# Attention and two feed-forward layers on one core: one cleared conversion tile, two score banks, and a new written order

## The chip, the cores and the metric

One core of a Trainium2 chip runs the whole program in one launch. The time is device microseconds from the first to the last instruction of an execution, as the chip reports it; three executions of the kernel before took 922.51, 922.75 and 926.28 us, and their median, 922.75 us, is the time before. The engines are TensorE (PE in the profile, its weight loads PEld), VectorE (DVE), ScalarE (ACT), GpSimd (POOL) and SyncE (SP), which issues the DMA transfers.

## The reference, cut to what matters

Inputs q, k and v are (4, 8, 576, 64) in f32. Attention masks by blocks of 64: a query sees every key of its own block and of the blocks before it. The 2304 rows of 512 that come out go through two feed-forward layers of width 2048.

```python
scores = scale * np.matmul(q, k.transpose(0, 1, 3, 2))
scores = np.where(block_i >= block_j, scores, -1e9)
attn = np.exp(scores - np.max(scores, axis=-1, keepdims=True))
attn = attn / (np.sum(attn, axis=-1, keepdims=True) + 1e-09)
x = np.matmul(attn, v)                       # then (B, S, H*D)
h = x @ w_in;  x = (h * np.tanh(softplus(h))) @ w_out      # layer 1 (Mish)
h = np.maximum(x @ w_in2, 0); out = (h * h) @ w_out2       # layer 2
```

## The kernel before

**Tiles and stages.** The 2304 rows are cut into six chunks of 384 (`CH1`). Chunks 0 and 1 hold the first 192 query positions of the four batches ("lo" attention, `attention_lo`, in f32); chunks 2 to 5 hold the other 384 positions of one batch each ("hi" attention, `attention_hi`, four pairs of heads per chunk, sixteen in all). A pass takes one chunk through one layer (`PASSES`): sixteen slices f of the hidden width, each with a first product (line 1206, into a bank `hp`), an activation, a rounding of the result into two f16 halves (`g_parts`), and a second product (line 1272, into four banks `acc`). Every f16 product is a sum of three matmuls, high by high, low by high and high by low. Pass (0, 0), the first one, runs in f32 instead (lines 1226 and 1241), so that it needs no halves of the weights.

**Weights.** A weight block of 128 x 1024 comes from DRAM 16 bits off its place (line 1053) and is put together in three steps by `decode`: GpSimd clears the target `wf` (line 1058), ScalarE or VectorE converts the upper 16 bits of each number from bf16 to f16 and writes them into the upper halves of the cleared words (lines 1060 and 1061), and VectorE shifts the middle bits by 13 and ORs them in (line 1062, `scalar_tensor_tensor`). There are 16 blocks in each layer. Those of layer 1 stay in tiles of their own (called `first`, `late` and `ws` in the profile), those of layer 2 go through a ring `wf` of three.

**Attention's score banks.** One PSUM tile of two banks (`spare`) holds the hi scores of a pair of heads, one head in each bank (line 833), and, in the last 64 columns of bank 0, small results: scales and norms (`sc`, `qm`, `sx`, `vm`). The lo heads of chunk 1 use the banks in turn (`s1`). For a hi tile VectorE takes the maximum of both heads in one instruction (line 843, `peak`), ScalarE takes the exponential of each head (line 851, `expo`), then P is scaled and rounded to f16 by ScalarE (line 870), VectorE takes the rest of the rounding (line 744), a DMA transposes both halves (line 874), and TensorE multiplies with v (line 931), in bank 0. For a lo head the maxima are lines 972 and 973, the negative scale 974, the exponentials 977, the row scaling 749 or 751, the transposes on TensorE 990 to 993, a copy 720 or 722, and the product with v 1005 and 1006.

**Order.** The program is a list of tasks, and each engine runs its own in a written order. `PLAN` is that list, packed: for every position the task (two bytes, as an offset) and the engine that runs it (one byte). A task with two or three possible engines (`choose`) takes the one that the plan names. The costs in `c_dve`, `c_act` and so on served the search for a plan and do nothing once there is one. Waits between engines are set from what a task reads and writes. SyncE issues the transfers in the plan's order too, so a transfer that waits for its buffer holds those behind it.

Of the kernel before, what the change touches and what calls it, by code (L numbers as in the profile page):

```python
# [59 lines left out]
def seg_len(tiles):  # L60
# [10 lines left out]
       "pn": A + V, "set": A + V, "ptc": A + V, "ph": A + V, "pl": P + V}  # L71
# [23 lines left out]
    "O-K9tG!5Agxm#mhbtj%a+jZ6*MBy==>Dp@v(l@Fbzc=95%~(84*YR1;>MeDz*0SzwyIogd&n&x63y{m%ExHyRe&+XE{P=)=;rb;}_`>R_DIWTaPa}P5pV|!T"
    "u20Zpwq2=-_Mp0Gw=U6lcxVScJYQc~d!484MBo#m`MGV@?K+v6r)#oR(KUL{s%w>&=p){BP!;u7Ro;w8i&J%`PEi|8vR-=I%BvM4Z`mwOWlj~1w-fcX#@TCp"
    "#@gq2;Y7V+BW#R)rE(h03eVUZcB=|&6u%?+JZ;nTx(z0C8WNG0?Q)Gk>Y)AA>T0wO+OyV5AL~sstF7VIOmA2{;=NT*G4dL@{DeKDK<o69J!(TVOb_G1Yw`1N"
    "yMP=UY7dfq9jq^rc+&bHz17ONXY`oeZGF&uJ=c|1%uUl`yNw;rCr`doA8TX3*nQT;YN(UVCjy`7NBahUPt-njw>kEA{XqPBX$Eh)*fn;&-qEqvgX>&tV&xdW"
    "1^;za8?xprS5nLLwJk-<Z_T^Qu)Yad+SIN@_r^BSE+pQKY^WA!tb5-Y*i*VvAKL?(t*3OcjkCAy2|Ym;g&sd&-SJ07eArhf@ca-tQjz#n)Q5QQOlI~`S-pTC"
    "Khzj9t~2vS+gR6v+3%=_dg?_h$om(pmhN>A+s)+qaO;mXrSuTzYJ_gq4DGj5_&#f$bgvC@gKU6R)(|~nZ@D(?`X^#`9n#mk3VPBWu!g!zFS-U=VP(|Q8Z)OZ"  # L100
    "T0F$HnJxo+ZnF*ev=iRFTr;gJ8P$c;c7u9x5>L~`dQ)|fX`x&3#I+i%Zni=_>=yeYS$4ASwkdX&KC`c_E#FggBRN@JpIZwn@9Jn4C$6QP<SroJk9TiaW9zA_"
    "@oiD;YJ!b7U~OrgqoZ`Wovjk&d2vnvej@j-vI6dMJkSb+Y-}G{Rn@mjD(9ZH%gC~eK#!{6S|ioAlfcxqc8*=hsjrBq-T)KoXuWEYGexoVOpxac^6P9nNA=05"
    "3%Fly!$6jEts2>UHt2T{oZDwaj#Uc~!77ZL#A;3*t)v}qd#sclvUcESo|WcX){0qE@TfSR>R|<~h&3bMZ?z1bX%6l^u2C9920y0Pu&zC5yU7M{;`+18RIWdf"
    "y)Tg^Ly61tdK$bK72!%PGOaRqcj^&*Jq3(@p6t1sTzix(ooEk(>|e0zW9p}J_PEB{Kv1VI(*3}pLgd*P*AL`)n#_8N43qBHaI~3bgRtmneQ%HIkbi@_nbuDu"
    "ZJ&Qg53$d8_NE5vIla!)cy{PQPETR|r@-4@>^+7oAFlh|?fSc|@Q-lc6`dFP3E<Z|Amkj*`$?e8mC-8w(D@$SX`?{8ndHq|@X2=`D~QNsPRC%RALN{W=3lkW"
    "`jgt}eQdgi`2%#5TDhU%S0C`9r|u*3o&d3XlKXw_N!_XnWO`#_{JcG)$MN_vWNK-!x+hq9vTjg6B66#H&Ta;q?jVx~Sre=ZXI(|^4gzJ)RTFiEUz+P4aOpM;"
    "09hM=#O*krO<|(CoQuBJ%Ia}KPK1e@AeZB$Gz04|hY7obGfi}<&bNl_KhG}Xlx*XSbO5t{BJ*yr_MGr8WWi<NdVAH<N;04Z*>tw9hEdVP8nA9FID9s`S63Cg"
    "S{K2yGsxlFh*cfcgPR)aHFCWMd~l&12mUrf>X1G|zN9WB7eCVkES^L5ovgE2v4pnTBvs}7O|$z|ll`jW`%5?x@4`f<V)rRl*^bv6c;f&uD@m50t_oI(yg3Wx"
    "D9yWqb_s|*7DTSDqO5QXnQ;)bE<tqvY)6sx#gN=ZwDLf-N0^_rET{8*6*dRY--&MCU!cukp;?~yeAjVuc5=RUlXv@VmoEyJHPd!q3ic_Wtvt`S_CC<_w#(N0"
    "@o4d`wZW&-O>U*_17RC!s<m}**&^SZ{C`kiz)&q+F=A0bvwcC%OIEY|`5<RUcOEFe24))%_Yb9l%ENcdt-cG{zph(?rWbQvXeF3E5)>=W?ls&TYKCjnfZxm9"  # L110
# [24 lines left out]
    "pxO|-IvP!t*osc78_}wzcU>F0sakr{6{8YtsT%ZQHB?&#$euH})`~i*da7&%3<C0J=_tCmlUU#UsoL+&SEMql2_trQ`}`BUk?pZcu<z}zKJ{D=SC88AXxrj9"
    "+bQZ#C$hnB_iwv`cAD0}U}tNP+u-;4U;UY|?NWa%9ncO|UQFFkMulL-(%R|g_&>mGW%ab%;?Lsyq}%9c_{MIKtKru9N8RPr`E9kzpXw^Rer|<d0spV@%lM^A"
    "_b0lm)XpvQf1vv)%l9I81-0L7#v7`k=K3=395>rna5Jc7XZdojgDcMc3?!!eQf``GOAj#9Petw<UleXyPPdVxx2WnCP=_DT=l&Dw6}eA+0e2j4{_eBxV_%tm"
    "Xum%620ztvA24>1%C3o<=nuehV}1PDO=q)<PIE8Z@s{6Bb+=0&+n@b@9S!?!u-E-&jiln(K_|4z3b?hLz~}voej`=z2A$znP{o&^bE`s)T+gjiVS246{0c3y"
    "b$ZM%r5_CYmVy2;YmCOrsm+ga1MEAxpFy1auj$Diu}4Al#(Ef@=w}1qld5hKoIcUb)CAYpK6V%DL-&I|cD;%Gdv3dt+5A?9A2)&KHMPM;yIbu$b+emo20d0c"
    "`x31E(0!*5Tt~RAGd2HwaBvdr@;7&*eWoGo{}sK>$JFfaf_1;Bt+lY%+y`LdKzEl-P)obY-hl-^fP=5Fx2bTO((g?G0WXE${-(=8_xHGt(G4J0eH*LqIZLC|"  # L140
    ")m_BcTv%|ey{tEMzCB@6)dV&^2gdlC>bwT0GW=h-7t|PuGwf8j=SAHIA1%=zVX_yf)$8)M5_mU+r;q5+Ugi4%y~r?iv2%IX*`5N=JK0&_dIv^M=W{>2bvpJ}"
    "hqL-|I){Ksk8*CR*pqYyRjohQ%62@xSRdBz%PD_8{GUB=z5>WNOcTMw+92<7JeB7A1=qfu%{%DTN?UPwqq7QG3C`^xMth-aSDphq$qF&njqaiZIFW%t9;Od!"
    "11}i8i}%;qjqseaj`Toz{(9y7USGsY*&ZtHf}nbF+u@soPt9}<cGu;cH>dY#jxGV**Mhao%Wi=)h9h&xH_$;JSRQND<8D7SdmVoF_)EZm`XJ#>-;fULMzCqC"
# [417 lines left out]
def tile_attention_moe(ctx, tc, qk, qp, va, vd, w1, w2, out):  # L561
# [31 lines left out]
    def fixed(tiles):  # L593
        return sch.ring(len(tiles), lambda i: tiles[i % len(tiles)])
# [184 lines left out]
    def clear():  # L779
# [3 lines left out]
        for z in zeros:  # L783
            for i in R["raw"].insts:
                z.deps.update(i.tasks)
# [810 lines left out]
```

## Time and profile before

| | |
|---|---|
| median of three executions | 922.75 us |
| the profiled execution | 925.42 us, span 923.6 us |
| busy TensorE / VectorE / ScalarE / GpSimd | 895.7 / 575.5 / 575.1 / 63.6 us |
| instructions on them | 5786 / 1432 / 1121 / 86 |
| mean granted TensorE clock | 0.992 of 2.4 GHz |
| DMA | 168.79 MB, 183 GB/s over the span |

A busy microsecond counts an instruction from its start to its end, and that includes time in which it stands on its engine and is held up. Starts are microseconds from the start of the span. In a list of groups the numbers behind the bar are busy us in all, mean ns of one, and the idle time before them with what ended it.

### The profile page before, as it was taken

The page shows a single profiled execution, that of the slowest core. Times are in us where ns is not written, and L with a number is a line of the kernel's source. Part 1 is how long each engine was busy: PE and PEld are TensorE (multiplying, and loading weights), DVE is VectorE, ACT ScalarE, POOL GpSimd, SP SyncE. Part 2 cuts the span into 40 slices and gives each one's busy share as a digit, 9 for nine tenths or more (in the row PEclk, how much of TensorE's full clock was granted, in tenths as well). Part 3 has the DMA queues.
Part 4 walks back from the last instruction along what each step waited for, and adds up shares of the span by engine and source line. Part 5 has one row for each costly group of instructions (what it writes and reads, how often), then busy time and mean ns, then how long its engine had stood idle before and what let it go on. Part 6 is the DMA issues. An engine that isn't in the chain of part 4 may idle for free. (4 is left out here: it accounts for less than half of the span.)

```text
span 923.6 us, 15581 instructions
## 1 busy us (share of the span) xinstructions
PE 895.7 (97%) x5786; PEld 533.2 (58%) x5786; DVE 575.5 (62%) x1432; ACT 575.1 (62%) x1121; POOL 63.6 (7%) x86
## 2 busy tenths in 40 slices
PE   4999999999999999999999999999999999999997
PEld 4666555555555555555566555555666666666664
DVE  6668999999989877586721686976531341331211
ACT  3988899999977655447322786987642333544442
POOL 6000201121211100010000000000000000000000
PEclk8899999999999999999999999999999999999999
DMA  7597556999688899738732388696732222343530
GB/s 272 205 362 288 176 159 156 310 291 290 248 299 198 263 231 234 223 107 199 245 98 83 108 224 211 180 241 160 161 101 70 69 69 69 115 137 137 171 114 35
DMA packets 141772, 168.79 MB, mean 183 GB/s; under 512 B 105856, under 2 KB 110976, under 8 KB 141696
## 3 DMA queue, kind: packets, MB, share of 16 engines
q1 hardware_dynamic: 141696, 167.79, 61.2%
q8 instruction: 45, 0.74, 0.3%
q14 instruction: 31, 0.25, 0.1%
HBM read 125.30 MB, written 17.30 MB: 154 GB/s over the span
## 5 line engine op out<-in xcount | busy, mean ns | idle before, releaser
L744 DVE SCALAR_TENSOR_TENSOR g<-h,cst,g 128x384 f16<-128x384 f32 x176 | 108.7, 619 | 222.4 <-ACT g L1034 218.1
L1212 ACT ACTIVATE h<-hp,cst 128x384 f32<-128x384 f32 x176 | 101.3, 577 | 216.9 <-PE hp L1206 205.7
L1272 PE MATMUL acc<-g,ws 128*128 128x384 f16 x1128 | 228.2, 326 | 0.0
L1272 PE MATMUL acc<-g,raw 128*128 128x384 f16 x984 | 205.2, 326 | 1.6 <-ACT ev L1285 1.6
L1206 PE MATMUL hp<-x,first 128*128 128x384 f16 x768 | 154.8, 326 | 1.0 <-ACT h L1212 0.9
L1272 PEld LDWEIGHTS <-ws 128*128 128x128 f16 x1128 | 108.7, 98 | 72.8 <-issue 2.2
L1272 PEld LDWEIGHTS <-raw 128*128 128x128 f16 x984 | 95.3, 98 | 65.5 <-issue 3.3
L1206 PEld LDWEIGHTS <-first 128*128 128x128 f16 x960 | 92.4, 98 | 63.8 <-issue 3.9
L1206 PE MATMUL hp<-x,raw 128*128 128x384 f16 x552 | 117.9, 326 | 0.0
L1034 ACT ACTIVATE g<-h,cst 128x384 f16<-128x384 f32 x119 | 72.8, 613 | 27.8 <-PE acc L1272 25.6
L1206 PEld LDWEIGHTS <-raw 128*128 128x128 f16 x648 | 61.6, 98 | 40.8 <-issue 1.9
L1206 PE MATMUL hp<-x,ws 128*128 128x384 f16 x408 | 84.7, 326 | 0.4 <-DMA ws<-wspill 0.4
L744 DVE SCALAR_TENSOR_TENSOR pb<-pad,st,pb 128x384 f16<-128x384 f32 (+2 forms) x96 | 71.1, 750 | 13.9 <-ACT pb L870 13.9
L870 ACT ACTIVATE pb<-pad,st 128x384 f16<-128x384 f32 (+2 forms) x96 | 66.4, 713 | 21.3 <-DVE st L863 6.4
L851 ACT ACTIVATE pad<-spare,st,sq 128x448 f32<-128x448 f32 (+1 forms) x96 | 65.1, 680 | 9.8 <-DVE st L846 4.7
L1206 PEld LDWEIGHTS <-ws 128*128 128x128 f16 x504 | 47.8, 98 | 30.8 <-DMA ws<-wspill 0.5
L843 DVE TENSOR_REDUCE st<-spare 128x2 f32<-128x896 f32 (+1 forms) x48 | 47.8, 996 | 10.3 <-PE spare L836 7.6
L1226 PE MATMUL hp<-xs,first 128*128 128x384 f32 x128 | 47.5, 491 | 0.0
L1206 PE MATMUL hp<-late,first 128*128 128x384 f16 x192 | 41.5, 326 | 0.0
L833 PE MATMUL spare<-q 64*128 64x448 f16 (+2 forms) x384 | 38.5, 306 | 1.5 <-ACT pad L851 1.1
L1217 ACT ACTIVATE h<-h 128x384 f32<-128x384 f32 x75 | 38.4, 514 | 0.6
L1241 PE MATMUL acc<-h,late 128*128 128x384 f32 x96 | 36.9, 495 | 0.2 <-ACT h L1231 0.2
(238 smaller groups left out, 1122.9 us busy)
## 6 DMA issues: line engine op xcount, KB each, us to landing
ws<-wspill SPq DMA_DIRECT2D x68, 512.0 KB, 4.6
raw<-wspill SPq DMA_DIRECT2D x68, 512.0 KB, 4.1
raw<-in_w_dram SPq DMA_DIRECT2D x27, 1023.8 KB, 6.5
wspill<-wn SPq DMA_DIRECT2D x24, 512.0 KB, 3.9
qk<-in_qp_dram SPq DMA_DIRECT2D x16, 480.0 KB, 4.6
vs<-in_va_dram SPq DMA_DIRECT2D x16, 320.0 KB, 4.1
pad<-in_w_dram SPq DMA_DIRECT2D x5, 1023.8 KB, 6.8
out_dram<-ev SPq DMA_DIRECT2D x24, 192.0 KB, 2.4
```

The costliest lines, as they stand in the source:

```text
L744: return sch.add("DVE", c_dve(n) + 62 * ap, lambda: nc.vector.scalar_tensor_tensor(dst(), a(), s() if ap else s, c(), op0, op1), r=r, w=w, ...
L833: nc.tensor.matmul(out=pp.t[:, hd, o:o + k1 - k0], lhsT=qh.t[rows, u, a:a + 128], rhs=qh.t[rows, w, nq + k0:nq + k1], start=p == 0, stop=p ...
L843: sch.add("DVE", c_dve(2 * (o1 - o0)), lambda: nc.vector.reduce_max(both(st, j, r0), pp.t[r0:, :, o0:o1], axis=AX.X), w=[(pp, 0), (st, j)])
L851: t = sch.add("ACT", c_act(o1 - o0, True, 3), lambda hd=hd: nc.scalar.activation(pf[hd].t[r0:, k0:k0 + o1 - o0], pp.t[r0:, hd, o0:o1], AF. ...
L870: sch.add("ACT", c_act(n, False, 1), lambda pb=pb, pv=pv, s=s: nc.scalar.activation(pb.t[:, 0:i + 1, 0, :], pv(), AF.Copy, scale=s()), r=[ ...
L1034: "ACT": ("ACT", c_act(n, False, 1), lambda: nc.scalar.activation(dst(0), src(), AF.Copy, scale=s()), False),
L1206: nc.tensor.matmul(out=hp.t[:, 0:n], lhsT=w.t[:, f % 2, a, 128 * k:128 * k + 128], rhs=x.t[:, c, k, 0:n], start=k == 0 and i == 0, stop=k ...
L1212: sch.add("ACT", c_act(n, True, 1), lambda: nc.scalar.activation(h.t[:, 0:n], hp.t[:, 0:n], (AF.Mish, AF.Relu)[l], scale=hs()), r=[(cst, ( ...
L1217: "ACT": ("ACT", c_act(n), lambda: nc.scalar.activation(hv(), hv(), AF.Square), False),
L1226: nc.tensor.matmul(out=hp.t[:, 0:n], lhsT=wf.t[:, 512 * (f % 2) + 128 * k:512 * (f % 2) + 128 * k + 128], rhs=xs.t[:, k, 0:n], start=k == ...
L1241: ts.append(sch.add("PE", c_mm(4 * n), lambda m=m, acc=acc: nc.tensor.matmul(out=acc.t[:, 0:n], lhsT=wf.t[:, 512 * (f % 2) + 128 * m:512 * ...
L1272: nc.tensor.matmul(out=acc.t[:, 0:n], lhsT=wo.t[:, f % 2, a, 128 * m:128 * m + 128], rhs=g.t[:, c, 0:n], start=f == 0 and i == 0, stop=f = ...
```

## The change

Four edits, and a new plan.

```diff
-       "pn": A + V, "set": A + V, "ptc": A + V, "ph": A + V, "pl": P + V}
+       "pn": A + V, "set": A + V, "ptc": A + V, "ph": A, "pl": P + V}
+    top = pad.bitcast(F32)[:, 2048:3072]
+    R["top"] = fixed([top])
...
-    spare = {"ab": psp.tile([128, 2, 512], F32, tag="pab", name="spare")}
-    R["sc"] = fixed([spare["ab"][:, 0, 448 + 4 * i:452 + 4 * i] for i in range(4)])
+    bank = [psp.tile([128, 512], F32, tag=f"bank{i}", name=f"bank{i}") for i in range(2)]
+    R["sc"] = fixed([bank[1][:, 448 + 4 * i:452 + 4 * i] for i in range(4)])
...
+    nc.gpsimd.memset(top, 0.0)
...
-        def peak(st, j, pp, r0, o0, o1):
-            sch.add("DVE", c_dve(2 * (o1 - o0)), lambda: nc.vector.reduce_max(both(st, j, r0), pp.t[r0:, :, o0:o1], axis=AX.X), w=[(pp, 0), (st, j)])
+        def peak(st, j, pp, o0, o1):
+            for hd in range(2):
+                t = sch.add("DVE", c_dve(o1 - o0), lambda hd=hd: nc.vector.reduce_max(st.t[:, 2 * j + hd:2 * j + hd + 1], pp.t[hd][:, o0:o1], axis=AX.X),
+                            w=[(pp, hd), (st, (j, hd))])
...
-                sch.add("ACT", c_act(n, False, 1), lambda pb=pb, pv=pv, s=s: nc.scalar.activation(pb.t[:, 0:i + 1, 0, :], pv(), AF.Copy, scale=s()),
-                        r=[(st, 7), f], w=[(pb, 0)])
+                choose(A + V, {
+                    "ACT": ("ACT", c_act(n, False, 1), lambda pb=pb, pv=pv, s=s: nc.scalar.activation(pb.t[:, 0:i + 1, 0, :], pv(), AF.Copy, scale=s()), False),
+                    "DVE": ("DVE", c_dve(n, True) + 62, lambda pb=pb, pv=pv, s=s: nc.vector.tensor_scalar(pb.t[:, 0:i + 1, 0, :], pv(), s(), None, ALU.mult), True)},
+                    [(st, 7), f], [(pb, 0)])
...
+        top = wf if l else R["top"].new()
+        high = lambda: top.t.bitcast(F16).rearrange("p (c two) -> p c two", two=2)[:, :, 1]
+        if l:
+            sch.add("POOL", 1000.0, lambda: nc.gpsimd.memset(wf.t, 0.0), w=[wf])
...
         sch.add("DVE", c_dve(n), lambda: nc.vector.scalar_tensor_tensor(
-            U(wf.t), mids(), 13, U(wf.t), ALU.logical_shift_right, ALU.bitwise_or), r=[raw], w=[wf], lock=True)
+            U(wf.t), mids(), 13, U(top.t), ALU.logical_shift_right, ALU.bitwise_or), r=[raw, top], w=[wf], lock=True)
```

The layer 1 blocks are converted in one tile `top`, cleared once, and the OR writes the result to its own place; layer 2 keeps its clears. The two score banks are two tiles; maxima and the copy of the tail (line 889) are one instruction per bank; the small results move to bank 1, the product with v stays in bank 0. P's rounding and the scaled copy of the product with v (line 944) may go to either engine.

The plan, unpacked byte by byte, says what it does with the choices. It has 4539 tasks (4491 before): 64 more maxima and tail copies, 16 clears fewer. GpSimd has 48 tasks (80 before), ScalarE 836 (871), VectorE 1541 (1426). Of the 96 roundings of P 24 go to VectorE (7 in chunk 2, 13 in chunk 3, 4 in chunk 4); the copies of line 944 all stay on ScalarE; of the conversions 8 go from ScalarE to VectorE and 2 back; of the row scalings of line 749 17 go to VectorE and 9 back. The changes between the exponential's and Mish's tables on ScalarE are 39 (41 before). Ahead of the first product of pass (0, 0) TensorE has 28 tasks (29 before), ScalarE 47 (57), VectorE 83 (76); GpSimd has seven: three of layer 2's clears and the four small ones of line 962, with the clear of `top` ahead of them (before: nineteen, fifteen of layer 1's clears and the four small ones). The first transposes of TensorE stand behind four score groups (five before).

## Rows read from the trace of the kernel before

**Rows 1.** The page: busy us by engine, and the granted clock in 40 slices.

```profile
PE 895.7 (97%) x5786; PEld 533.2 (58%) x5786; DVE 575.5 (62%) x1432; ACT 575.1 (62%) x1121; POOL 63.6 (7%) x86
...
PEclk8899999999999999999999999999999999999999
```

**Rows 2.** Stages: us, then busy us (count) of PE, PEld, DVE, ACT, POOL, PEclk, DMA share, GB/s.

```profile
11.20:19.30 8.10, 0.00 (x0) 0.00 (x0) 6.21 (x15) 3.81 (x18) 3.80 (x5) 0.75 0.97 375
19.30:29.00 9.70, 9.65 (x40) 8.14 (x41) 3.75 (x19) 7.03 (x30) 0.00 (x0) 0.50 0.35 121
29.00:41.70 12.70, 11.63 (x92) 8.44 (x91) 11.02 (x42) 11.79 (x41) 0.00 (x0) 1.00 0.51 182
41.70:75.00 33.30, 33.04 (x149) 20.55 (x148) 23.82 (x54) 30.01 (x63) 0.00 (x0) 1.00 0.91 338
75.00:225.00 150.00, 147.11 (x867) 84.65 (x866) 143.13 (x343) 140.41 (x236) 23.98 (x30) 1.00 0.80 237
225.00:325.00 100.00, 96.22 (x649) 55.15 (x648) 89.69 (x233) 78.14 (x134) 14.68 (x17) 1.00 0.78 245
325.00:576.00 251.00, 248.31 (x1733) 146.07 (x1730) 157.48 (x408) 133.25 (x272) 5.45 (x7) 1.00 0.66 179
576.00:910.00 334.00, 334.00 (x2182) 198.31 (x2182) 132.42 (x312) 166.04 (x327) 5.03 (x7) 1.00 0.43 125
```

**Rows 3.** Order of time, 6.5 to 15.5 us: start, us, engine, line, what, idle before.

```profile
6.80 8.22 DVE L974 TENSOR_SCALAR st<-st 128x3 f32<-128x3 f32 x1
...
9.58 3.63 POOL L1058 MEMSET first<- 128x1024 f32 x4
...
14.05 0.95 POOL L1058 MEMSET first<- 128x1024 f32 x1
15.12 0.42 ACT L977 ACTIVATE pt<-acc,st 128x192 f32<-128x192 f32 x1 [13.11 <-DVE st L973]
```

**Rows 4.** Order of time on PE alone, 10 to 42 us.

```profile
10.90 0.22 PE L968 MATMUL hp<-never,above 128*128 128x128 bf16 x1
19.35 0.45 PE L990 MATMUL acc<-ident,pt 128*128 128x128 f32 x1 [8.23 <-ACT pt L749]
...
20.23 1.81 PE L967 MATMUL acc<-vs 128*128 128x192 f32 x6
...
30.52 0.98 PE L967 MATMUL spare<-vs 128*128 128x192 f32 x6
...
41.72 1.51 PE L1226 MATMUL hp<-xs,first 128*128 128x384 f32 x4
```

**Rows 5.** Groups of POOL by line and shape: busy us, mean ns, idle before.

```profile
L1058 POOL MEMSET first<- 128x1024 f32 x8 | 7.4, 951 | 0.0
```

**Rows 6.** The same of VectorE.

```profile
L843 DVE TENSOR_REDUCE st<-spare 128x2 f32<-128x896 f32 x32 | 34.7, 1083 | 3.6 <-PE spare L833 1.9 <-PE spare L836 1.2 <-PE spare L807 0.5
...
L1036 DVE TENSOR_SCALAR g<-h,cst 128x384 f16<-128x384 f32 x39 | 16.4, 423 | 14.8 <-PE acc L1272 9.7 <-ACT xs L944 4.0 <-PE spare L1147 0.9
...
L843 DVE TENSOR_REDUCE st<-tl 128x2 f32<-128x256 f32 x16 | 6.6, 410 | 0.0
...
L1061 DVE CAST wf<-raw 128x1024 f16<-128x1024 bf16 x4 | 3.0, 746 | 0.5 <-POOL wf L1058 0.5
```

**Rows 7.** The same of ScalarE.

```profile
L870 ACT ACTIVATE pb<-pad,st 128x512 f16<-128x512 f32 x32 | 22.3, 713 | 5.9 <-DMA late<-pb 2.5 <-ACT pad L851 2.0 <-DMA pt<-pb 0.8
...
L1060 ACT ACTIVATE wf<-raw 128x1024 f16<-128x1024 bf16 x12 | 16.2, 1352 | 0.8 <-DMA raw<-in_w_dram 0.7
```

**Rows 8.** Waits of PE over the span: us in total, times, longest.

```profile
PE spare L833 <- ACT pad L851: 1.1, 1, 1.1
...
PE spare L1077 <- ACT pad L851: 0.7, 2, 0.4
```

**Rows 9.** Order of time on VectorE alone, 33 to 36 us.

```profile
33.59 0.16 DVE L974 TENSOR_SCALAR st<-st 128x3 f32<-128x3 f32 x1
...
33.97 1.20 DVE L1062 SCALAR_TENSOR_TENSOR first<-raw,first 128x1024 uint32<-128x1024 uint32 x1
```

More of the change, by code (lines that the diff above doesn't have):

```diff
@@ L95 @@
[L95 to L98, printed above, removed]
@@ L170 @@
+    "{<jG5+eH6Ql9kH2;a7-#)V|mXkw=q8Cdvwz8@Y6(my8!OF7+GfN4nAf^ex@5A@tWPNA8!26E*Ye8@gOOlk2gPppBT1x@25HBikOq>_4i@e`>|WU2U`)XX%mn"
+    "{NL2%zghUdzCTiYV>QX8%zpu>c1Zg"
 )
@@ L783, in clear @@
         for z in zeros:
-            for i in R["raw"].insts:
+            for i in R["raw"].insts + R["top"].insts:
                 z.deps.update(i.tasks)
@@ L832, in mm @@
                         rows = slice(64 * hd, 64 * hd + 64)
[L833 removed]
+                        nc.tensor.matmul(out=pp.t[hd][:, o:o + k1 - k0], lhsT=qh.t[rows, u, a:a + 128], rhs=qh.t[rows, w, nq + k0:nq + k1],
                                          start=p == 0, stop=p == 2 and not mask)
                 for hd in range(2 if mask else 0):
[L836 removed]
@@ L838, in scores @@
-            steps.append(sch.add("PE", 3 * (c_mm16(k1 - k0) + 16) + (110.0 if mask else 0.0), mm, r=[(qh, (p, j)) for p in range(2) for j in range(2)], w=[(pp, 0)]))
+                    nc.tensor.matmul(out=pp.t[hd][:, o + k1 - k0 - 64:o + k1 - k0], lhsT=above, rhs=never[:, 0:1].to_broadcast([128, 64]), start=False, stop=True)
+            steps.append(sch.add("PE", 3 * (c_mm16(k1 - k0) + 16) + (110.0 if mask else 0.0), mm, r=[(qh, (p, j)) for p in range(2) for j in range(2)], w=[(pp, 0), (pp, 1)]))
@@ L886, in attention_hi @@
                 steps.append(halves(vs, v3, sv, R["vm"].new()))
-            peak(st, 0, pp, 0, 0, n)
+            peak(st, 0, pp, 0, n)
             if i == 2:
-                sch.add("DVE", c_dve(256), lambda pp=pp, n=n: nc.vector.tensor_copy(tail.t, pp.t[:, :, n:n + 128]), w=[(pp, 0), tail])
-                peak(last, 1, tail, 0, 0, 128)
-            low(st)
+                for hd in range(2):
+                    t = sch.add("DVE", c_dve(128), lambda pp=pp, n=n, hd=hd: nc.vector.tensor_copy(tail.t[:, hd], pp.t[hd][:, n:n + 128]), w=[(pp, hd), (tail, hd)])
+                    t.banks = (hd,)
+                sch.add("DVE", c_dve(256), lambda: nc.vector.reduce_max(both(last, 1), tail.t, axis=AX.X), r=[(tail, 0), (tail, 1)], w=[(last, 1)])
+            low(st, [(st, (0, 0)), (st, (0, 1))])
             expo(st, 4, pp, 0, 0, n, pf, 0)
@@ L918, in second @@
             step.rows = 0.86
-            settle(lambda: av.t[:, 0, 0:nq], av, nq, x, hp, xo, sv)
+            settle(lambda: av.t[0][:, 0:nq], av, nq, x, hp, xo, sv)
+            for t in av.tasks:
+                t.banks = (0,)
             return [step]
@@ L1497, in tile_attention_moe @@
             for _ in range(t.fillers or 0):
-                nc.tensor.matmul(out=spare["ab"][:, 1, 448:512], lhsT=ones, rhs=ones[:, 0:64], start=True, stop=True)
+                nc.tensor.matmul(out=bank[1][:, 448:480], lhsT=ones, rhs=ones[:, 0:32], start=True, stop=True)
             t.fn()
```

197 lines of the change are left out of this document (100 added, 97 removed).

## The prediction, made before the changed kernel ran

> **What bounds the kernel now.** I read the page first, then the stages, then single instructions in order of time. On the page TensorE is busy 895.7 of 923.6 us [rows 1]: the change takes no matmul away, so it can win only TensorE's 27.9 us of idle time and whatever ran at the lower clock. The stages say where that lies. From 576 to 910 us TensorE is busy all the time, and from 325 to 576 us it lacks 2.7 us; between 11.2 and 19.3 us it does nothing at all; from 75 to 225 us it lacks 2.9 and from 225 to 325 us 3.8, with VectorE busy 143.1 of 150 and 89.7 of 100 us and ScalarE 140.4 and 78.1 [rows 2]. So there is one large hole, at the start, and a long stretch in which three engines are full together.
>
> The order of time shows what the hole is. VectorE starts the tiny instruction of line 974, three numbers in each partition, at 6.80 us and it stands for 8.22 us; ScalarE's first exponential waits for VectorE until 15.12 us [rows 3]. The same instruction takes 0.16 us later on [rows 9]. While it stands, GpSimd clears conversion targets, one 0.95 us clear after another, and it ends at 15.02 us, when the last of that run ends (14.05 + 0.95) [rows 3]. TensorE has finished its scores at 11.12 us and stands until 19.35 us [rows 4].
>
> **The change part by part.**
>
> *Layer 1's clears go.* Each costs GpSimd 0.95 us [rows 5], or 0.91 in a run (3.63 for four [rows 3]). By the unpacked plan fifteen leave the start and four come (`top` and three of layer 2), so GpSimd is through 11 x 0.91 = 10 us earlier, at 5.0 us, 1.8 us before VectorE reaches line 974. That instruction then costs 0.16: gain 8.22 - 0.16 = 8.06 us for ScalarE's first exponential (7.06) and, behind it, the first transposes (11.29, 0.2 us after TensorE's last score of today's order). If the margin of 1.8 us is eaten, one more clear costs 0.9.
>
> The Trainium skill's page "SBUF — State Buffer", section "Who interferes with whom", has a rule against so long a wait: GpSimd and a VectorE instruction in a two-port mode exclude each other, and the one that comes first holds the shared pair for its whole instruction. By that, VectorE would have got in behind one clear, after 0.95 us at most, and the gain here would be about 0.8. The trace disagrees: the instruction stood past the ends of the nine clears of that run (four of them and the last are in [rows 3]).
>
> *The clock at the start.* After TensorE's standstill its clock is at the lower level, 1.2 GHz, from 19.3 to 29.0 us (granted 0.50 [rows 2]); six score matmuls take 1.81 us there and 0.98 at 2.4 GHz [rows 4]. Without the standstill I expect the upper level to hold. TensorE's 9.65 us would be 5.2, a gain of at most 4.4; but ScalarE has 7.03 us to do in that stretch [rows 2] and becomes the next limit, so 2.7 at most from the rows. Between 0 and 4.4 I take 2.0, near ScalarE's bound.
>
> *The next limit at the start.* The weights could be late. The first block's OR ends at 35.17 us (33.97 + 1.20 [rows 9]) and TensorE uses it at 41.72 [rows 4], 6.55 us later. The transfers have room ahead of that: DMA share 0.35 and 0.51 from 19.3 to 41.7 us, and 0.91 after it [rows 2]. With one `top`, convert and OR run by turns: 1.35 at most [rows 7] + 1.20, 2.6 us per block and 41 us for sixteen, within the time in which they come. I put the cost at nothing; if decoding didn't move forward with the rest, 10.1 - 6.55 = 3.5 us.
>
> *Work on VectorE.* A maximum of 128x896 takes 1083 ns and one of 128x256 410 [rows 6], so 1.05 ns a column and 0.14 us fixed: 64 more instructions are 9.0 us, an upper bound, since neighbours overlap. P's rounding takes ScalarE 0.713 us at 512 columns [rows 7]; on VectorE the nearest rows are 0.423 at 384 and 0.746 at 1024 [rows 6], so 0.49: 24 roundings are +11.8 there and -17.1 on ScalarE. Six conversions net are +4.5 on VectorE and -8.1 on ScalarE. Some 22 small moves (row scalings, roundings of x and g) at 0.42 are another 9. In sum VectorE gets some 34 us and loses the 8.1 of standstill, ending near 601 us; ScalarE ends near 547; GpSimd, with sixteen clears (15.2 us) and sixteen other tasks fewer, near 37: it would be 48.4 if those cost nothing and 33.2 if each cost as much as a clear.
>
> How much of it is on the path? 20 of the 24 roundings (9.8 us) and half of the splits (4.5) lie in chunks 2 and 3, about 75 to 325 us, where VectorE has 17.2 us of room in 250 [rows 2]. Nothing of it is on the path while TensorE's queue hides it; all of it, 14.3, if VectorE is the limit there. ScalarE is freed by the same roundings, and GpSimd, whose 38.7 us there [rows 2] could hold VectorE up as at the start, gets up to sixteen tasks fewer. At the other end TensorE's whole idle time of these stages, 6.7 us, could go. Between -6.7 and +14.3 I take +1, near zero, for the load is put mostly where VectorE has room.
>
> *Two tiles for two banks.* The waits of TensorE on a score bank that the split could take away are 1.1 and 0.7 us [rows 8]: 1.8 at most, counted within that range. The copies of line 944 do not move: nothing.
>
> **Sum.** -8.06 - 2.0 + 1 = -9.1 us. The profiled execution took 925.42 us (span 923.6), so 916.3; the median of the runs is 2.67 lower, so 913.7 us by the measure that counts.
>
> **Rivals.**
> 1. *VectorE becomes the bound in chunks 2 and 3, by half:* +7 in place of +1, 919.7 us. For it: it has 143 of 150 us there today. Against it: ScalarE, which works ahead of VectorE in each pair of roundings, loses 14.3 us there (20 x 0.713).
> 2. *VectorE becomes the bound in both attention stretches: slower.* All 14.3 us of 75 to 325, and in chunks 4 and 5 another 4.5 of splits and 2.0 of roundings, and the new order's row scalings and x roundings (9) with them: +29.8, less 8.06 of the start, with the clock staying low: 944.5 us; with half of it, 929.6, which is where I put it. It decides from the point where VectorE has no idle time left from 75 to 325 us. Against it: the freed ScalarE, with 2 table changes fewer, feeds it sooner.
> 3. *The clears weren't what held line 974.* Were it the rule quoted above, something else ended at 15.0 us, and the start stays: -0.8 + 1, 922.9 us. Against it stands the coincidence of 15.02 with 15.00 us, and the 0.16 us of the same instruction without clears beside it.
> 4. *The middle gains as well:* the 6.7 us of idle time there go, and 1 us of load doesn't come: 906 us. For it: ScalarE's relief and the split banks. Against it: VectorE has no room to speed up.
>
> **How the numbers follow.** My case 0.66 (913.7, by itself 908 to 917.5), rival 1 0.12, rival 2 0.04, rival 3 0.06, rival 4 0.12. A measurement tells 0.5%, 4.6 us, from no change: faster is under 918.1, slower over 927.4. Faster: 0.66 + 0.12 + a third of rival 1 = 0.82. Same: the rest of rival 1 and rival 3 = 0.14. Slower 0.04. The range of 906 to 920 leaves out rivals 2 and 3, a third of rival 1 and the lower half of rival 4, some 0.2.
>
> **What would show it.** Line 974's first instance at 0.2 us in place of 8.22; ScalarE's first exponential near 7.1 us; the first transposes near 11.3; TensorE with no standstill over 2 us before the first f32 product, which starts at 31 to 34 in place of 41.72; a granted clock of 1.00 between 19 and 29 us. VectorE's busy sum near 601, ScalarE's near 547, GpSimd's near 37. TensorE's idle time from 75 to 325 us within 2 us of 6.7. I am wrong if the first product moves up and the time doesn't (then VectorE took it back, and its share from 75 to 325 is over 98%), or if line 974 still stands for microseconds.

## The result, and the profile after

The changed kernel took 911.84 us (median of four executions, 909.52 to 912.44) against 922.87 us for the kernel before (four executions, 922.51 to 926.28): 11.0 us less. The ratio of their means, as all ratios below, is 0.9868, with a 95% interval of [0.9838, 0.9897]. The profiled execution took 911.32 us (span 909.5), 14.1 less than that of before. The two differences are not the same because the profiled execution of before lies 2.6 us above its median and this one 0.5 us below; the spread of before comes up again below.

The page of the kernel after, busy time by engine and the granted clock, against [rows 1]: 3.9 us less on TensorE, 12.1 more on VectorE, 20.4 less on ScalarE, 25.5 less on GpSimd.

```profile
PE 891.8 (98%) x5786; PEld 530.5 (58%) x5786; DVE 587.6 (65%) x1547; ACT 554.7 (61%) x1084; POOL 38.1 (4%) x55
...
PEclk9999999999999999999999999999999999999999
```

The stages of the kernel after, in the same stretches and columns as [rows 2]:

```profile
11.20:19.30 8.10, 7.96 (x63) 7.23 (x64) 7.01 (x38) 7.30 (x30) 0.00 (x0) 1.00 1.03 402
19.30:29.00 9.70, 9.70 (x73) 6.91 (x71) 9.01 (x34) 9.46 (x39) 0.00 (x0) 1.00 0.90 330
29.00:41.70 12.70, 12.70 (x62) 8.09 (x61) 10.78 (x24) 10.67 (x24) 0.00 (x0) 1.00 0.90 330
...
75.00:225.00 150.00, 146.47 (x897) 83.15 (x896) 144.80 (x377) 138.65 (x219) 21.47 (x27) 1.00 0.83 240
225.00:325.00 100.00, 98.86 (x681) 58.06 (x679) 91.38 (x248) 75.47 (x138) 10.30 (x13) 1.00 0.84 244
```

The hole of 11.2 to 19.3 us is gone (7.96 us busy in place of none), the clock of 19.3 to 29.0 is 1.00 in place of 0.50, and from 75 to 325 us TensorE lacks 3.5 + 1.1 = 4.7 us where it lacked 6.7.

The order of time at the start of the kernel after, all engines, answers to [rows 3]; line 974 is now 990, the exponential 993.

```profile
4.22 0.95 POOL L1076 MEMSET wf<- 128x1024 f32 x1
6.03 0.56 DVE L988 TENSOR_REDUCE st<-acc 128x2 f32<-128x384 f32 x1 [4.76 <-PE acc L984]
...
6.75 0.17 DVE L990 TENSOR_SCALAR st<-st 128x3 f32<-128x3 f32 x1
7.02 0.42 ACT L993 ACTIVATE pt<-acc,st 128x192 f32<-128x192 f32 x1 [5.00 <-DVE st L990]
```

The last clear ends at 5.17 us, before VectorE comes to its line, which takes 0.17 in place of 8.22. TensorE alone, against [rows 4]:

```profile
11.34 0.30 PE L1006 MATMUL acc<-ident,pt 128*128 128x128 f32 x1 [0.84 <-DVE st L990]
11.80 0.98 PE L983 MATMUL hp<-vs 128*128 128x192 f32 x6
...
27.91 1.46 PE L1244 MATMUL hp<-xs,first 128*128 128x384 f32 x4
```

The transposes come 8.0 us earlier, the first f32 product 13.8 us earlier (27.91 against 41.72), and from that product to the end it is 881.6 us against 881.9. So the start holds nearly the whole gain. Single products further on say less, because the two orders put other work between them: the 33rd matmul of pass (0, 0) is 11.9 us earlier, the last one 14.0, the first f16 product of a pass 11.0, and the end 14.1 again.

### The profile page after: what moved, and what is told of

Read it like the earlier page. It is cut to its first block, busy times and chain, and to the rows that moved or that the text cites. A ratio compares the mean times of both kernels' runs of the same rounds, so it can differ in the third digit from the quotient of the medians.

```text
span 909.5 us, 15587 instructions
## 1 busy us (share of the span) xinstructions
PE 891.8 (98%) x5786; PEld 530.5 (58%) x5786; DVE 587.6 (65%) x1547; ACT 554.7 (61%) x1084; POOL 38.1 (4%) x55
## 5 line engine op out<-in xcount | busy, mean ns | idle before, releaser
L1050 ACT ACTIVATE g<-h,cst 128x384 f16<-128x384 f32 x113 | 69.2, 612 | 15.6 <-PE acc L1290 13.7
L859 ACT ACTIVATE pad<-bank,st,sq 128x448 f32<-128x448 f32 (+1 forms) x96 | 65.0, 679 | 20.3 <-DVE st L853 17.2
L879 ACT ACTIVATE pb<-pad,st 128x640 f16<-128x640 f32 (+2 forms) x72 | 50.9, 722 | 19.7 <-DVE x L748 4.4
L848 DVE TENSOR_REDUCE st<-bank 128x1 f32<-128x448 f32 (+1 forms) x96 | 52.6, 575 | 10.9 <-PE bank L837 5.1
L1244 PE MATMUL hp<-xs,first 128*128 128x384 f32 x128 | 49.7, 495 | 0.0
L837 PE MATMUL bank<-q 64*128 64x448 f16 (+2 forms) x384 | 40.5, 306 | 2.7 <-ACT pad L859 1.4
L1052 DVE TENSOR_SCALAR g<-h,cst 128x384 f16<-128x384 f32 x49 | 20.3, 416 | 31.8 <-PE acc L1290 27.7
```

The lines of the kernel that those rows point to most:

```text
L837: nc.tensor.matmul(out=pp.t[hd][:, o:o + k1 - k0], lhsT=qh.t[rows, u, a:a + 128], rhs=qh.t[rows, w, nq + k0:nq + k1], start=p == 0, stop=p ...
L848: t = sch.add("DVE", c_dve(o1 - o0), lambda hd=hd: nc.vector.reduce_max(st.t[:, 2 * j + hd:2 * j + hd + 1], pp.t[hd][:, o0:o1], axis=AX.X) ...
L859: t = sch.add("ACT", c_act(o1 - o0, True, 3), lambda hd=hd: nc.scalar.activation(pf[hd].t[r0:, k0:k0 + o1 - o0], view(hd)[r0:, o0:o1], AF. ...
L879: "ACT": ("ACT", c_act(n, False, 1), lambda pb=pb, pv=pv, s=s: nc.scalar.activation(pb.t[:, 0:i + 1, 0, :], pv(), AF.Copy, scale=s()), False),
L1050: "ACT": ("ACT", c_act(n, False, 1), lambda: nc.scalar.activation(dst(0), src(), AF.Copy, scale=s()), False),
L1052: "DVE": ("DVE", c_dve(n, True) + 62, lambda: nc.vector.tensor_scalar(dst(0), src(), s(), None, ALU.mult), True)},
```

## The experiments

Three questions: is it the clears that hold line 974, and what do they cost; what are the clock and the new order worth at the start; and what do the split banks and VectorE's roundings do in the middle. The experiments ran on three chips, with the kernel before beside them on each: 923.58 us beside e1 to e4 (914.92 to 927.54, 25 executions), 923.23 beside e5 to e8 (920.47 to 926.99, 13) and 923.6 beside e9 to e12 (914.09 to 927.73, 18). The kernel after has only the four executions above; e8 is the nearest to it among the experiments.

### e1 and e12: the changed kernel with the clears back

```diff
     with tc.manual_schedule():
+        for k, j in [(1, 4), (1, 5), (1, 0), (0, 6), (0, 5), (1, 1), (0, 0), (1, 3), (0, 3), (0, 1), (0, 2)]:
+            nc.gpsimd.memset(R["f32", k, j].insts[0].t, 0.0)
         for t in seq:
```

Eleven clears of layer 1's targets, at the head of GpSimd's queue, in the order of the kernel after.

> The changed kernel with eleven of layer 1's clears put back at the head of GpSimd's queue (the targets are written in full later, so nothing else changes). Theory (the run of clears holds VectorE's tensor_scalar until the run ends): GpSimd is busy until about 15 us, line 990's first instance stands some 8 us in place of 0.17, the first exponential goes from 7.02 to about 15.1, the first f32 product from 27.91 to 36 or later, TensorE's clock falls to 1.2 GHz behind the standstill, and the time is 919 to 924 us. Rival (one clear can hold VectorE for at most its own 0.95 us): line 990 stands at most 1 us and the time is 911 to 913 us.

> The same kernel as e1, one more profiled execution, for the same question: by the theory the tiny VectorE instructions stand for 0.5 to 1 us in some executions (as in e1's profile, span 912.7) and for 5 us and more in others (span 917 and over); by the rival they stand for one clear at most each time in this kernel, and its span is again within 1 us of 912.7.

Measured in e1: 919.18 us (914.52 to 921.82, nine executions), ratio to before 0.995 [0.992, 0.9979]. Its profiled execution was its fastest, 914.52 (span 912.7). e12 is one more execution of the same kernel, 922.09 us (span 920.3). The order of time at the start, first e1:

```profile
6.56 0.95 POOL L1515 MEMSET late<- 128x1024 f32 x1
...
6.81 0.73 DVE L990 TENSOR_SCALAR st<-st 128x3 f32<-128x3 f32 x1
7.46 0.97 POOL L1515 MEMSET first<- 128x1024 f32 x1
7.64 0.42 ACT L993 ACTIVATE pt<-acc,st 128x192 f32<-128x192 f32 x1 [5.62 <-DVE st L990]
...
8.38 0.95 POOL L1515 MEMSET late<- 128x1024 f32 x1
...
8.89 0.46 DVE L996 TENSOR_SCALAR st<-st 128x3 f32<-128x3 f32 x1 [0.29 <-ACT pt L993]
...
9.59 1.77 DVE L755 TENSOR_SCALAR pt<-pt,st 128x192 f32<-128x192 f32 x2
...
32.51 1.46 PE L1244 MATMUL hp<-xs,first 128*128 128x384 f32 x4
```

and then e12:

```profile
6.55 0.95 POOL L1515 MEMSET late<- 128x1024 f32 x1
6.79 8.23 DVE L990 TENSOR_SCALAR st<-st 128x3 f32<-128x3 f32 x1
...
14.05 0.95 POOL L1076 MEMSET wf<- 128x1024 f32 x1
15.12 0.42 ACT L993 ACTIVATE pt<-acc,st 128x192 f32<-128x192 f32 x1 [13.11 <-DVE st L989]
...
37.41 1.46 PE L1244 MATMUL hp<-xs,first 128*128 128x384 f32 x4
```

The same program, with the clear beside it started within 0.01 us and the instruction within 0.02 us of the other execution, went two ways. In e1 VectorE gets in when the clear ends that was running (6.56 + 0.95 = 7.51 against 6.81 + 0.73 = 7.54), and so again at the next one (8.38 + 0.95 = 9.33 against 8.89 + 0.46 = 9.35); in e12 it gets in only when GpSimd has no clear left, at 15.02 us, as in [rows 3]. The `tensor_scalar`s still pay in e1, some 0.2 to 0.8 us each, and the granted clock is 0.58 between 11.2 and 19.3 us, where the kernel after has 1.00: the first f32 product is at 32.51 us, 4.6 later than without the clears, and the end 3.2 later. In e12 it is at 37.41, 9.5 later, and the end 10.8 later. So in the new order the clears cost 3 us in one profiled execution and 11 in the other; by the median of e1's and e12's ten executions (919.6) it is 7.8. The eight that weren't profiled took 916.12 to 921.82 us, so ways in between are likely too.

The Trainium skill's page "SBUF — State Buffer", section "Who interferes with whom", says that whichever of the two engines issues first holds the shared pair for its whole instruction. e1's profile agrees (one clear, 0.73 us); e12's and that of before don't (8.23 and 8.22).

### e11: the kernel before, once more

> The kernel before, one more profiled execution. Theory (whether VectorE gets in between two of GpSimd's clears is a matter of chance or of phase): line 974 stands for 0.2 to 8.3 us; where it is under 2 us, the span is under 918, where it is over 6, it is over 920. Rival (it always stands through the run of clears, and the kernel's spread from 915 to 928 us comes from elsewhere): over 6 us here, whatever the span.

One execution, 925.73 us (span 924.0):

```profile
6.79 8.23 DVE L974 TENSOR_SCALAR st<-st 128x3 f32<-128x3 f32 x1
```

This one fits both the theory and the rival. What decides between the two ways is not shown: e1 and e12 are one program, but ran on two chips. The chip alone doesn't settle it, for on e1's chip line 974 of e4 (below) stood 8.30 us; but no single kernel was seen to go both ways on one chip. That the executions of before at 914.09, 914.92 and 916.27 us are ones in which VectorE got in is likely by their times, but none of them was profiled: it isn't shown.

### e2: line 974 as another kind of instruction

```diff
-        sch.add("DVE", 72.0, lambda: nc.vector.tensor_scalar(st.t[:, 4:7], st.t[:, 0:3], -scale, None, ALU.mult),
+        sch.add("DVE", 72.0, lambda: nc.vector.tensor_tensor(st.t[:, 4:7], st.t[:, 0:3], minus, ALU.mult),
```

The kernel before, with a tile of three constants as second input.

> The kernel before with one instruction changed: the negative scale of line 974 is a tensor_tensor with a tile of three constants in place of a tensor_scalar; the clears stay. Theory (it is the kind of VectorE instruction that the clears hold up): line 974 takes about 0.2 us and the first exponential starts near 7.1 us, but the next tensor_scalar (line 980, behind the exponentials) then stands until 15.0 us; the first transposes move from 19.35 to about 16.5 to 17.5, and the time falls by 1 to 4 us, to 919 to 922. Rival (VectorE waits for something else that comes at 15.0 us): line 974 or its successor still ends at 15.0 us, the exponential starts at 15.1 and the time stays at 922.9.

Measured: 922.14 us (914.99 to 925.91, twelve executions), ratio 0.9965 [0.994, 0.9991]. VectorE and GpSimd in order of time (line 974 is 976, line 980 is 982, the clear 1060):

```profile
6.74 0.95 POOL L1060 MEMSET first<- 128x1024 f32 x1
6.89 0.16 DVE L976 TENSOR_TENSOR st<-st,minus 128x3 f32<-128x3 f32 x1
...
8.58 6.46 DVE L982 TENSOR_SCALAR st<-st 128x3 f32<-128x3 f32 x1
8.70 6.34 DVE L976 TENSOR_TENSOR st<-st,minus 128x3 f32<-128x3 f32 x1
...
14.06 0.96 POOL L1060 MEMSET first<- 128x1024 f32 x1
15.07 0.18 DVE L984 RECIPROCAL st<-st 128x3 f32<-128x3 f32 x1
```

The same three numbers take 0.16 us as `tensor_tensor`, inside one of the same clears (6.74 to 7.69 us). The next `tensor_scalar` in the queue takes the stand over, 8.58 to 15.04 us, again to the end of the last clear (14.06 + 0.96), and the 8.70 instruction stands only behind it. So in this execution it is this kind of instruction that waits for GpSimd, and the wait moved one instruction on: the first f32 product and the end came 3.3 and 3.1 us earlier. The first transposes came at 17.81 us, somewhat later than expected. The Trainium skill's page "SBUF — State Buffer", section "Who interferes with whom", says that a VectorE instruction with two SBUF inputs contends with a GpSimd instruction that reads SBUF, not with one that only writes it. The row of line 976 at 6.89 us agrees, taking a clear as one that only writes.

### e3 and e10: the old order without the run of clears

```diff
-        sch.add("POOL", 1000.0, lambda: nc.gpsimd.memset(wf.t, 0.0), w=[wf])
+        sch.add("POOL", 1000.0, lambda: nc.gpsimd.memset(wf.t, 0.0) if l or (k, j) == (1, 7) else None, w=[wf])
...
+        early = [R["f32", k, j].insts[0] for j in range(NF // 2) for k in (0, 1) if (k, j) != (1, 7)]
+        for i, inst in enumerate(early):
+            if i % 5 in (0, 3):
+                nc.gpsimd.memset(inst.t, 0.0)
+            elif i % 5 in (1, 4) or i == 2:
+                nc.scalar.activation(inst.t, ones[:, 0:1].to_broadcast([128, 1024]), AF.Copy, scale=0.0)
+            else:
+                nc.vector.memset(inst.t, 0.0)
```

The kernel before, its fifteen early clears shared out: six on GpSimd, three on VectorE, six on ScalarE, all at the start.

> The kernel before, its own order and its one-tile banks, with the fifteen early clears shared out: six on GpSimd, three on VectorE and six on ScalarE, all ahead of the first scores' results. Theory (the clears alone make the start): first exponential at 7 to 8 us, TensorE's standstill gone, clock at 2.4 GHz from 19 to 29 us, first f32 product at 29 to 33.5 us, time 910 to 914 us, as good as the changed kernel. Rival (the new order, the split banks and the engines' new shares bring a part of it): the start moves by 8 us and the time stays at 915 us or over.

> The same kernel as e3, beside e9 on the same chip: 913 to 916 us, as in its first call, and line 974's first instance again under 1 us.

Measured: 914.5 us (912.95 to 916.07, six executions), ratio 0.9889 [0.9867, 0.991]; in e10 913.6 (913.12 to 916.23, seven), ratio 0.991 [0.9875, 0.9945]. e3 in order of time:

```profile
6.81 0.19 DVE L974 TENSOR_SCALAR st<-st 128x3 f32<-128x3 f32 x1
8.66 0.40 ACT L977 ACTIVATE pt<-acc,st 128x192 f32<-128x192 f32 x1
...
31.11 1.19 PE L1226 MATMUL hp<-xs,first 128*128 128x384 f32 x3
```

The old order, old bank and old roundings, without the wait: 9 to 10 of the 11 us are there. e3 lies between the theory's 910 to 914 and the rival's 915. The spread is 3 us in each, where the kernel before has 6 to 14; but e9, below, has the same clears and a spread of 6, so the wait is not the only source of it. ScalarE's own clears hold its first exponential back to 8.66 us (7.02 in the kernel after), and still the first f32 product is 10.6 us earlier than before.

### e4: the clock alone

```diff
+NFILL = 38
...
+            if t.eng == "PE" and t.group == ("att", 0, 0) and t.fn.__name__ == "turn":
+                for _ in range(NFILL):
+                    nc.tensor.matmul(out=spare["ab"][:, 1, 0:448], lhsT=ones, rhs=ones[:, 0:1].to_broadcast([128, 448]), start=True, stop=True)
```

The kernel before, with TensorE busy on throw-away products while it stands; the wait stays.

> The kernel before with 38 matmuls of 448 columns on TensorE, whose result nobody reads, in its standstill from 11.1 to 19.3 us; the clears and VectorE's wait stay. Theory (the lower clock behind the standstill costs 2 to 4.4 us of its own): the clock stays at 2.4 GHz from 15 to 29 us, the first f32 product comes at 37.3 to 39.7 us in place of 41.72, time 918.5 to 921. Rival (ScalarE is as late as TensorE there, the clock costs nothing): the clock stays up and the product stays at 41 to 42 us, time 922.9.

Measured: 927.35 us (925.16 to 931.9, twelve executions), ratio 1.0046 [1.0021, 1.0071]. The stages of e4,

```profile
11.20:19.30 8.10, 7.87 (x44) 4.06 (x42) 6.21 (x15) 3.81 (x18) 3.80 (x5) 1.00 0.99 367
19.30:29.00 9.70, 9.64 (x75) 8.20 (x77) 7.67 (x36) 9.57 (x42) 0.00 (x0) 1.00 0.43 149
```

line 974 (975 here) and the first f32 product

```profile
6.73 8.30 DVE L975 TENSOR_SCALAR st<-st 128x3 f32<-128x3 f32 x1
...
37.93 1.51 PE L1227 MATMUL hp<-xs,first 128*128 128x384 f32 x4
```

and TensorE's waits of e4 from 430 to 700 us:

```profile
PE acc L1273 <- ACT ev L1286: 3.5, 2, 2.5
PE spare L932 <- DMA late<-pb: 2.2, 2, 1.5
```

The clock held at its upper level, 2.4 GHz (granted 1.00 in both stretches, where [rows 2] has 0.75 and 0.50), and the first f32 product came at 37.93, 3.8 us earlier: by this run that is what the lower clock cost up to there in the old order. But it doesn't reach the end. From 441 us on the lead is lost, in waits that the kernel before has too, only shorter (1.6 and 0.4 us in the same stretch), and in a fall of the granted clock to 0.50 for 3.4 us behind the longest of them, at 457 us; the end is 2.0 us later than before. In e3 and in the kernel after, ScalarE and VectorE gained as much at the start as TensorE, and there the lead held. That TensorE's lead alone runs into what the other two deliver is read from these waits and not tested by itself; why it overshoots by 2 us is open.

### e8: eight matmuls before the first scores

```diff
+        for _ in range(8):
+            nc.tensor.matmul(out=bank[0][:, 0:448], lhsT=ones, rhs=ones[:, 0:1].to_broadcast([128, 448]), start=True, stop=True)
         for t in seq:
```

> The changed kernel with eight more matmuls of 128x448 on TensorE ahead of its first scores, whose results are overwritten; the rest as it is. Theory (what is left of the start's loss is the lower clock on the first scores, about 1 us): the granted clock is at the upper level from about 6 us on, six score matmuls before 11 us take 0.98 us in place of 1.81, the first f32 product starts 0.5 to 1.5 us earlier than 27.91, and the time is 909.5 to 911.5. Rival (the start hangs on ScalarE's and VectorE's chain, not on the scores): the clock rises and the first product stays within 0.3 us of 27.9; time unchanged, 911 to 912.5.

Measured: 910.84 us (909.73 to 912.38, four executions), ratio 0.9864 [0.984, 0.9887]. TensorE in order of time:

```profile
4.02 1.90 PE L983 MATMUL acc<-qk 128*128 128x192 f32 x6
5.81 1.10 PE L983 MATMUL acc<-qk 128*128 128x192 f32 x6
...
27.69 1.46 PE L1244 MATMUL hp<-xs,first 128*128 128x384 f32 x4
```

The second score group takes 1.10 us where it took 1.91 in the kernel after, and the first f32 product is 0.22 earlier: the rival's outcome, by which the start hangs on the chain of ScalarE and VectorE. The time can't be told from the kernel after's; no better version came of it.

### e5: all roundings of P on ScalarE

```diff
-                choose(A + V, {
+                choose(A, {
```

> The changed kernel, with all 24 roundings of P that its plan gives to VectorE put on ScalarE instead, at the same places of the order. By the rows ScalarE gets 24 x 0.713 = 17.1 us more (to about 572) and VectorE loses some 24 x 0.49 = 11.8 (to about 576). Theory (neither engine is TensorE's bound in chunks 2 and 3, so the place of a rounding is worth nothing): TensorE's idle time from 75 to 325 us stays within 2 us of 4.7, and the time within 911 to 914 us. Rival (VectorE's help there is what kept the middle from losing): ScalarE is full from 75 to 225 us, where it has 11 us of room for 13 of these roundings (9 us), TensorE's idle time there grows by 3 us or more, and the time is 915 to 920. Other rival (VectorE was the limit): 907 to 910.

Measured: 914.51 us (913.41 to 916.44, six executions), ratio 0.9902 [0.988, 0.9924]. The middle in one stretch, first the kernel after:

```profile
75.00:325.00 250.00, 245.33 (x1576) 141.21 (x1575) 236.18 (x624) 214.12 (x356) 31.77 (x39) 1.00 0.84 242
```

and e5:

```profile
75.00:325.00 250.00, 243.96 (x1537) 139.29 (x1537) 229.16 (x599) 218.87 (x367) 31.05 (x39) 1.00 0.81 240
```

TensorE's idle time grows by 1.4 us, within the 2 of the theory, and matmul by matmul e5 is 3.5 us behind the kernel after at 75 us, 5.1 at 121, 6.4 at 250, 3.95 at 400 and 3.4 from 600 us on: in this trace what the roundings' place costs the middle is won back by the end. The time is 2.7 us over the kernel after's all the same, and 3.7 over e8's, which ran beside it; it is just past the theory's 914 and short of the rival's 915. What the profiled execution (915.72) lost, 3.5 us at the first f32 product, it lost before any of these roundings, because its matmuls stayed longer at the slower of the two paces of [rows 4] (1.81 and 0.98 us for six score matmuls). The granted clock doesn't show that: it reads 1.00 from the first matmul on in both traces. The durations do. The third score group of e5 took

```profile
8.11 1.97 PE L983 MATMUL acc<-vs 128*128 128x192 f32 x6 [0.27 <-DMA vs<-in_qk_dram]
```

and that of the kernel after

```profile
7.59 1.13 PE L983 MATMUL acc<-vs 128*128 128x192 f32 x6
```

The score group behind the first transposes still takes 1.81 us in e5, and 0.98 in the kernel after. Nothing in the edit reaches that place. Whether the other executions lost their time there too isn't known; I count the 2.7 us as unexplained.

### e6 and e7: the two banks as one tile again

```diff
-    bank = [psp.tile([128, 512], F32, tag=f"bank{i}", name=f"bank{i}") for i in range(2)]
+    whole = psp.tile([128, 2, 512], F32, tag="bank", name="bank")
+    bank = [whole[:, i, :] for i in range(2)]
```

e6 is this alone, in the new order; e7 has each pair of maxima and of tail copies in one instruction as well.

> The changed kernel with its two score banks as one tile again, so that whoever writes one bank waits for the readers of both; maxima and order stay as they are. Theory (the split was worth at most the 1.8 us of waits that the trace of before shows): 911 to 914 us, and the waits of TensorE on a score bank grow by 1 to 3 us in all. Rival (the new order leans on the split): these waits grow by more than 5 us and the time is 916 or more.

> As the kernel with one tile, and each pair of maxima is one instruction over both banks again, and each pair of tail copies too: 64 instructions fewer on VectorE. From 1.05 ns a column and 0.14 us fixed this takes 64 x 0.14 = 9 us from VectorE's busy time at most, 6 where neighbours overlap. Theory (VectorE isn't TensorE's limit): within 1.5 us of the kernel with one tile alone. Rival (VectorE is the limit from 75 to 325 us): 3 to 6 us faster than that kernel.

Measured: e6 929.94 us (925.77 to 931.15, eight executions), ratio 1.0062 [1.0041, 1.0083]; e7 929.8 (927.77 to 932.32, six), ratio 1.0067 [1.0045, 1.0088]. The rival of e6 was right: 18 us, more than the whole gain of the change. A stretch of pass (0, 0), all engines, first the kernel after:

```profile
32.35 0.55 PE L1021 MATMUL bank<-pt,pb 128*64 128x192 f32 x4
32.46 0.56 DVE L988 TENSOR_REDUCE st<-bank 128x2 f32<-128x384 f32 x1 [0.28 <-PE bank L984]
...
34.45 0.98 PE L983 MATMUL bank<-vs 128*128 128x192 f32 x6
```

and e6:

```profile
33.44 0.56 DVE L989 TENSOR_REDUCE st<-bank 128x2 f32<-128x384 f32 x1 [1.22 <-PE bank L1023]
...
36.43 1.08 PE L984 MATMUL bank<-vs 128*128 128x192 f32 x6 [1.68 <-ACT pt L994]
```

With two tiles the maximum starts when its own scores are there, while TensorE still works on the other bank; with one it waits for that work to end, and TensorE's next scores wait for an exponential that reads the other bank. TensorE's waits of e6 from 28 to 195 us, where the largest of them lie:

```profile
PE bank L984 <- ACT pt L994: 3.4, 2, 1.8
PE bank L1096 <- ACT pad L860: 1.6, 1, 1.6
PE bank L838 <- ACT xs L960: 1.2, 1, 1.2
```

The profile is 8.3 us behind the kernel after's at the last f32 product and 15 at the end. Taking 64 instructions off VectorE (e7) brings 0.1 us: in that kernel these instructions weren't on the path. The Trainium skill's page "PSUM — Partial Sum Buffer", section "PSUM bank collisions raise a hardware error", gives guarding by bank as the simple version of its rule. What guarding two banks as one costs is measured here.

### e9: the split banks in the old order

```diff
-    spare = {"ab": psp.tile([128, 2, 512], F32, tag="pab", name="spare")}
+    bank = [psp.tile([128, 512], F32, tag=f"bank{i}", name=f"bank{i}") for i in range(2)]
...
+                sch.add("DVE", c_dve(2 * (o1 - o0)), lambda: [nc.vector.reduce_max(st.t[:, 2 * j + hd:2 * j + hd + 1], pp.t[hd][:, o0:o1], axis=AX.X) for hd in range(2)], w=[(pp, 0), (st, j)])
```

e3's kernel with two tiles, and two maxima at the place of one.

> The kernel before with its early clears spread over three engines (e3) and, in the same written order, its score bank as two tiles of one bank each, as in the change: each fused maximum and tail copy becomes two instructions, one per bank, at the same place. Compare with e3 itself in this call. Theory (the split is worth nothing until the order uses it: the old order keeps the small results and the products with v behind both banks anyway): within 3 us of e3, a gain of at most the 1.8 us of bank waits, less up to 6 us that 64 more instructions cost VectorE where they are on the path; 913 to 918. Rival (the split itself carries the 15 to 18 us that one tile cost the new order): 897 to 905.

Measured: 915.54 us (913.95 to 919.91, twelve executions), ratio 0.9923 [0.9899, 0.9947], beside 913.6 of e10: 1.9 us slower by the medians, with ranges that overlap. Busy time on the page of e10:

```profile
PE 891.2 (98%) x5786; PEld 529.1 (58%) x5786; DVE 569.9 (63%) x1434; ACT 580.8 (64%) x1128; POOL 54.8 (6%) x77
```

and on that of e9:

```profile
PE 896.0 (98%) x5786; PEld 531.2 (58%) x5786; DVE 574.1 (63%) x1498; ACT 580.8 (63%) x1128; POOL 55.5 (6%) x77
```

Sixty-four instructions more cost VectorE 4.2 us of busy time, and the old order gets nothing for them. e9's profiled execution, 919.11, is one of its two slowest: its granted clock is 0.84 from 19.3 to 29.0 us, where e10's is 1.00, with no clears beside it. The split is worth nothing by itself, and the new order is worth less than nothing without it. Whether the two together are worth anything is not settled: the kernel after (911.84) is 1.8 to 2.7 us ahead of e10 and e3, but the intervals of the three ratios, [0.9838, 0.9897], [0.9875, 0.9945] and [0.9867, 0.991], overlap. By these runs, the old kernel with its early clears shared out has the change's gain but for that.

## Why the prediction was right

**The lock was the step that counted, and its size was right.** Predicted: line 974 at 0.16 us, first exponential at 7.06, transposes at 11.29, GpSimd through at 5.0. Measured: 0.17, 7.02, 11.34 and 5.17. e12 puts the clears back and the 8.23 us return, and e3 takes the run of clears out of the old kernel and the wait is gone (0.19 us); e2 shows that it is the instruction's kind that GpSimd holds off. Rival 3, that something else ended at 15.0 us, falls.

**What I said against the Trainium skill's page was too strong.** The trace of before did contradict "one clear at most", but e1's execution agrees with it (0.73 us). A gain read from one profiled execution is the gain against that execution: 14.1 us between the profiled executions, 11.0 between the medians.

**The clock: the term of 2.0 us was mis-sized.** e4 gives it by itself in the old order: 3.8 us at the first f32 product, over my bound of 2.7 from ScalarE and inside that of 4.4 from TensorE. The 2.7 took ScalarE's busy time in one stretch as fixed; in e4 ScalarE did 9.57 us of work there in place of 7.03, work that had lain behind the stretch's edge. e3 fits the size: its first exponential is 6.5 us earlier than before's, its first f32 product 10.6, so 4.1 more. A third term was missing: by subtraction 13.8 - 8.1 - 3.8 = 1.9 us that the new order wins up to the first f32 product, so that this product came at 27.91 and not at 31 to 34. It may be no more than a shift, as TensorE has one task less ahead of that product (28 against 29).

**The weights: nothing predicted, nothing seen.** The first block's OR ends at 24.46 us (23.25 + 1.21), 10.7 earlier than in the kernel before, and from 12 to 60 us TensorE waits for no weights.

**The middle: +1 predicted, -0.3 measured** from the first f32 product to the end. TensorE's idle time from 75 to 325 us fell by 2.0 us, the edge of what I allowed. VectorE did not become the bound (rivals 1 and 2): it is busy 236.2 of 250 us, and 7 us less of busy time there (e5) made nothing faster; nor did 64 instructions less (e7), though that was tried only in e6's slower kernel.

**The split: "1.8 at most" was the right price in the wrong order.** It holds in the old order (e9: nothing gained). In the new order the two tiles carry 18 us (e6). Waits in the trace of before price an edit only while the order stays; here the order was made for the edit, and taking each part alone doesn't add up to the whole.

**VectorE's sum: 587.6, not 601.** The 64 more instructions cost 4.2 us (e9 against e10), not the 9.0 of the upper bound that I put in the sum, and the 24 roundings 10.6 (587.6 against 577.0 in e5), not 11.8. With the conversions at 4.5, about 1 us is left by subtraction for the small moves that I put at 9. ScalarE came to 554.7: the terms that I named give 549.9, not 547, and the roundings freed 13.6 us (568.3 in e5), not 17.1. GpSimd came to 38.1 (37). In the middle no run shows one of the three as the limit.

**Sum.** -9.1 predicted for the profiled execution, -14.1 measured. The three misses, 1.8 on the clock, 1.9 on the order and 1.3 in the middle, all point the same way and make up the 5.0. That the time itself came within 1.9 us (913.7 against 911.84) is in part luck: I took 2.67 off because the profiled execution of before lies above its median, and that of the kernel after lies 0.5 below its own. e12 stands between the two kernels: 3.3 us from before to it (order, split and roundings), 10.8 from it to the kernel after (the clears, with the clock behind them). By medians it is 3.2 to 4.0 and 7.8; by e3 and e10, 9 to 10 for the wait, with the clock behind it, in the old order.

## What to carry to other kernels

Look for tiny instructions with long bars: here a `tensor_scalar` of three numbers that took 8 us stood behind a run of GpSimd's clears, and spreading that run over three engines brought 9 to 10 us, nearly all that the whole rearrangement did. Where executions of one kernel spread by a per cent, profile it more than once before pricing a stall from it. And don't price a part of a change together with an order made for it: try the part in the old order and its absence in the new one.

## What the runs showed of the hardware that I had not expected

- A `tensor_scalar` of 128x3 on VectorE that comes up during a run of GpSimd's clears got in after one clear in one execution (0.73 us, e1) and past the whole run in others (8.22, 8.23 and 8.23 us in before, e11 and e12; 8.30 in e4; 6.46 in e2). The starts in e1, before, e11 and e12 lie within 0.02 us. What decides is not shown.
- A `tensor_tensor` of the same size, inside one of the same clears, took 0.16 us (e2).
- TensorE's pace does not rise at the same moment in each execution of nearly the same start: the third group of scores took 1.13 us in the kernel after and 1.97 in e5, behind two groups of 1.91 to 1.97 us in both. The granted clock reads 1.00 throughout in both traces, so at the start it has to be checked against durations.
